# Three chained stages on one core: layer 2 of the last stage moved, tile by tile, between layer 1's products

## The chip, the cores and the metric

One core of a Trainium2 chip runs the whole program in one launch. The metric is device time in microseconds (us). TensorE (PE) multiplies, VectorE (DVE) and ScalarE (ACT) move and combine data, GpSimd (POOL) combines data and issues one of the DMA queues, SyncE (SP) issues the other. An engine works through its instructions in the order of the program.

## The reference, cut to what matters

```python
x = attention(q_l, k_l, v_l, q_g, k_g, v_g)       # 4 x 544 tokens = 2176 rows of 512
x = x + gate * (relu(x @ w1[e]) @ w2[e])           # one of 8 experts e per row, some rows skipped
out = ((x @ w_a) * (x @ w_b)) @ w_out              # 512 -> 1536 -> 512: the stage that is changed
```

Everything is float32. The last line is the last stage; a float32 product is made there of three products of a high and a low part (high by high, high by low, low by high).

## The kernel before

Attention and routing run first, then the experts, then the last stage (class `Late`), which begins at about 307 us of the span and fills the rest. It runs under a schedule written out by hand, so the order of every engine's instructions is that of the code.

The last stage holds the 1536 hidden columns in 12 slices of 128. Six groups g take two slices each (`NM` is 12). Within a group four steps go over four blocks of rows (`TILES`: three of 4 tiles of 128 rows, and block 3 with 5), in the order 0, 1, 2, 3 in even groups and 3, 2, 1, 0 in odd ones. A step (`step`) makes the layer 1 products by seven half-size products per slice in place of eight (a Strassen-like scheme): product numbers 0, 4, 5, 1, 6, 2, 3, each for the slices j = 0 and 1, and each six matmuls into one of three PSUM banks per slice. Between them ACT copies a bank (`cp`, line 562) and DVE adds and multiplies (lines 590, 603, 598), and the result goes as high and low parts into the four tiles `g` (lines 562 and 594). The first two steps of group 0 are plain products (`plain_step`).

Layer 2 (`second`, line 516) multiplies the `g` tiles of the step before by the two slices of `w_out` (tiles `wo`, high and low), six 512-column matmuls for each 128 rows of output, into one of two PSUM banks (`accs`). ACT copies the bank to an `o` buffer (line 519), and the buffer goes to `out`: in group 0 by a plain store on SP's queue, in the later groups by an adding DMA on POOL's queue (line 524). In `step` all tiles of the step before are made one behind the other, between product 4 and product 5 (hook `P5`, then `s0` to `s3`, then `s`). There are two `o` buffers until the end of step 2 of group 1, where `all_o` adds four in the tiles `raws[3]` and `raws[4]`.

`aux(g, s)` says what else is issued at each hook (`P0`, `P1`, ... name the product that comes next): `conv` unpacks a loaded slice of weights (three DVE instructions, lines 317 to 319) and issues the next load on SP; `sums` (three DVE instructions) and `hi`, `lo` make the seven weight combinations in high and low parts; `wo_hi`, `wo_lo` do that for `w_out`; `turns` transposes rows on PE through the `accs` banks and `build` (`x_parts`) makes the seven combinations of a block's rows. Blocks 0 and 3 share one slot, so they are written to memory (`spill_x`, SP's queue: all of block 3 at `P5` of step 3 of group 0, all of block 0 at the end of step 2 of group 1) and read back (`fill_x`, POOL's queue) in groups 2 to 5: three pieces in step 1, at `s`, `P2` and `end`, the fourth at `s` of step 2. The block read back is used in step 3.

Of the kernel before, what the change touches and what calls it, by code (L numbers as in the profile page):

```python
# [8 lines left out]
F32 = mybir.dt.float32  # L9
# [5 lines left out]
ALU = mybir.AluOpType  # L15
# [210 lines left out]
class Late:  # L226
# [8 lines left out]
    def __init__(self, ctx, tc, dram, ident, wa, wb, wo, x2d, out, st):  # L235
        self.ctx, self.tc, self.nc = ctx, tc, tc.nc
        self.ident, self.x2d, self.out, self.st = ident, x2d, out, st
        self.src = (wa, wb, wo)
        self.es = ExitStack()
        self.xd = {b: [dram.tile([128, 7, 2 * self.NW[b]], F32, name=f"xd{b}{z}") for z in "hl"] for b in (0, 3)}  # L240
        self.todo = [(m, k) for g in range(0, self.NM, 2) for m, k in ((g, 0), (g, 1), (g + 1, 0), (g + 1, 1), (g, 2), (g + 1, 2))]
        self.ready, self.rows = [], {}
        self.nraw = self.nout = self.npair = 0

    def pool(self, name, es=None):
        return (es or self.es).enter_context(self.tc.tile_pool(reuse_waits="tile", name=name, bufs=1))

    def open_shared(self):

        self.xr_p = self.es.enter_context(self.tc.tile_pool(reuse_waits="tile", name="xr", bufs=6))  # L250
        p = self.pool("late_g")
        self.g = [p.tile([128, 640], F32R, name=f"g{z}") for z in range(4)]
        self.tmp = [p.tile([128, 640], F32, name=f"tmp{z}") for z in range(2)]
        self.idf = p.tile([128, 1], F32, name="idf")

    def open_first(self):

# [29 lines left out]
        self.xf_es.close()  # L287
        self.slots.append(self.slot(self.pool("late_w2"), 2))

    def all_o(self):  # L290
        self.o += [self.raws[3 + z // 2][:, 512 * (z % 2):512 * (z % 2) + 512] for z in range(4)]


    def fetch(self, raw, m, k):
# [186 lines left out]
            else:  # L481
                tt(a12, a12, a11, ALU.subtract)

    def spill_x(self, b):
        for z, x in enumerate(self.xview(b)):
            for a, e in ((0, 3), (3, 7)):
                self.nc.sync.dma_start(self.xd[b][z][:, a:e], x.bitcast(F32)[:, a:e].rearrange("p a k n -> p a (k n)"))

    def fill_x(self, b, z, a, e):
        x = self.xview(b)[z]  # L490
# [7 lines left out]
    def product(self, j, m, b, wp, xp, bank, start):  # L498
# [4 lines left out]
        for z, (w, x, k) in enumerate(terms):  # L503
            self.nc.tensor.matmul(bank[:, 0:n], lhsT=w[:, k], rhs=x[:, xp, k], start=start and z == 0, stop=z == 5,  # L504
                                  skip_group_check=not start)

    def second(self, b, g):

        nc = self.nc
        for q, t in enumerate(self.TILES[b]):  # L510
            acc = self.acc()
            for j in range(2):
                gh, gl = (x[:, 128 * q:128 * q + 128] for x in self.g[2 * j:2 * j + 2])
                wh, wl = self.wo[j]
                for z, (a, w) in enumerate(((gh, wh), (gh, wl), (gl, wh))):
                    nc.tensor.matmul(acc, lhsT=a, rhs=w, start=(j == 0 and z == 0), stop=(j == 1 and z == 2))  # L516
            o = self.o[self.nout % len(self.o)]
# [35 lines left out]
    def step(self, g, b, prev, run):  # L553
# [60 lines left out]
    def aux(self, g, s):  # L614
# [21 lines left out]
        more = 2 * g + 2 < self.NM  # L636
        c0, c1 = slice(0, 128), slice(128, 256)
        if (g, s) == (0, 0):
            add("p00", conv, conv)
            add("p01", do(self.turn_plain, 1, 0), do(self.turn_plain, 1, 1))  # L640
            add("p10", wo_hi, do(self.turn_plain, 1, 2), do(self.turn_plain, 1, 3), do(self.load_x, 2), do(self.sums, 0))
            add("p11", *his[2:])
            add("end", wo_lo, *los[2:])
        elif (g, s) == (0, 1):
            add("p0", *turns(2, 0, 1))
            add("p00", *turns(2, 2, 3), do(self.load_x, 3))
            build(2, ("p00", "s0", "s1", "s2", "s3", "p01", "p10"))
            add("p01", do(self.sums, 1))
            add("p10", *his[2:])
            add("p11", *los[2:])  # L650
        elif (g, s) == (0, 2):
            add("P0", *turns(3, 0, 1))
            add("P1", *turns(3, 2, 3))
            add("P5", *turns(3, 4), do(self.load_x, 1))
            build(3, ("P5", "s0", "s1", "s2", "s3", "s", "P6"))
            add("P6", conv)
            add("P2", conv)
        elif (g, s) == (0, 3):
            add("P5", do(self.open_slot2), do(self.spill_x, 3), sums)
            add("s0", *his)  # L660
            add("s1", *los)
            add("s2", conv)
            add("s3", conv)
            add("s", sums)
            add("P6", H(0, 1), H(4, 5), H(5, 6))
            add("P2", L(0, 1), L(4, 5), L(5, 6), H(1, 2))
            add("P7", L(1, 2), H(6, 7))
            add("P3", H(2, 3))
        if g and s == 0:
            add("P1", H(3, 4))  # L670
            add("P5", L(6, 7), L(2, 3))
            add("s0", L(3, 4))
            if g < 3:
                add("s3", conv)
                add("s4" if g == 1 else "s3", conv)
            add("s", wo_hi)
            add("P6", wo_lo)
        if (g, s) == (1, 0):
            add("P0", *turns(1, 0, 2, w=128, xf=0))
            build(1, ("P1", "P5", "s0", "s1", "s2", "s3", "s4"), c0, 0)  # L680
            add("end", do(self.load_x, 0))
        elif (g, s) == (1, 1):
            add("P0", *turns(1, 1, 3, w=128, xf=0))
            build(1, ("P1", "P5", "s0", "s1", "s2", "s3", "s4"), c1, 0)
            add("s3", *turns(0, 0, w=128, xf=1))
            add("s4", *turns(0, 2, w=128, xf=1))
            build(0, ("s", "P6", "P2", ((1, 2), "P1"), ((1, 2), "P5"), ((1, 2), "s0"), ((1, 2), "s1")), c0, 1)
        elif (g, s) == (1, 2):
            add("P1", *turns(0, 1, 3, w=128, xf=0))
            build(0, ("s0", "s1", "s2", "s3", "s", "P6", "P2"), c1, 0)  # L690
            add("s", conv)
            add("P6", conv)
            add("end", do(self.spill_x, 0), do(self.all_o))
        elif (g, s) == (1, 3):
            add("P1", sums)
            add("P5", *his)
            add("s0", *los)
            add("s1", conv)
            add("s2", conv)
            add("s3", sums)  # L700
            add("s", H(0, 1), H(4, 5))
            add("P6", L(0, 1), L(4, 5), H(5, 6))
            add("P2", L(5, 6), H(1, 2))
            add("P7", L(1, 2), H(6, 7))
            add("P3", H(2, 3))
        if g > 1 and more:
            if s == 1:
                add("P5", conv)
                add("s0", conv)
                add("s1", sums)  # L710
                add("s2", *his)
                add("s3", *los)
            elif s == 2:
                add("P5", conv)
                add("s1", conv)
            elif s == 3:
                add("P0", sums)
                add("P1", H(0, 1))
                add("P5", H(4, 5))
                add("s0", L(0, 1), L(4, 5))  # L720
                add("s1", conv)
                add("s2", conv)
                add("P6", H(5, 6))
                add("P2", L(5, 6), H(1, 2))
                add("P7", L(1, 2), H(6, 7))
                add("P3", H(2, 3))
        if g > 1 and s in (1, 2):
            for k, z, a, e in (("s", 0, 0, 3), ("P2", 1, 0, 3), ("end", 0, 3, 7)) if s == 1 else (("s", 1, 3, 7),):
                add(k, do(self.fill_x, (3, 0)[g % 2], z, a, e))
        return A  # L730

    def run(self):
        nc, tc = self.nc, self.tc
        with ExitStack() as ps:
# [3 lines left out]
            self.bk = [(bank[2], bank[0], bank[3]), (bank[6], bank[1], bank[4])]  # L738
            self.accs, self.nacc = (bank[5], bank[7]), 0
            self.zeroed, self.A = False, {}  # L740
            prev = None
            for g in range(self.NM // 2):
                for s, b in enumerate(self.ORDER[g % 2]):
# [897 lines left out]
```

## Time and profile before

| | us |
|---|---|
| median of 3 runs (759.27 to 761.83) | 760.81 |
| the profiled execution, its own time | 761.96 |
| its span | 760.2 |
| PE busy in the span | 705.7 (93%) |
| DVE, ACT, POOL busy | 470.9, 401.9, 170.0 |

The span runs from the first to the last instruction, and all positions below are us from its start. PE is busy for 93% of it, but the share is a mean over stages: the stretches in which PE stood still, and what ended each of them, say where time can go. The granted clock of PE is 1.00 at its full level and 0.50 at its half.

### The profile page before, as it was taken

How to read it: one execution, taken by the hardware profiler on the slowest of the kernel's cores; microseconds unless marked ns; L12 is line 12 of the kernel's file. 1: busy time of each engine (PE TensorE's matmuls, PEld its weight loads, DVE VectorE, ACT ScalarE, POOL GpSimd, SP SyncE). 2: the span in 40 equal slices, each digit the busy share in tenths (PEclk: the TensorE clock that was granted, in tenths of full speed). 3: DMA queues.
4: the chain of work that ended last, by engine and by line, in shares of the span. 5: the costliest groups of instructions: out<-in, count | busy, mean ns of one | idle time of the engine just before them, and what ended most of it. 6: DMA issues, size and time to landing. Idle time of an engine off the chain costs nothing.

```text
span 760.2 us, 14495 instructions
## 1 busy us (share of the span) xinstructions
PE 705.7 (93%) x5362; PEld 628.1 (83%) x5364; DVE 470.9 (62%) x1288; ACT 401.9 (53%) x994; POOL 170.0 (22%) x206
## 2 busy tenths in 40 slices
PE   8999998989989999889789889998999999999993
PEld 6887886868879888678689778997999899999982
DVE  6777886756565787676767469645465657533221
ACT  6776676616555784366365445534443444444332
POOL 3002022821343452000000112231222113222311
PEclk9999999899999999999989999999999999999997
DMA  9687633869977837732834478795659649745964
GB/s 302 201 252 237 204 129 111 265 222 371 370 253 247 270 107 241 242 111 98 324 107 160 68 150 269 165 314 141 106 120 277 170 58 293 161 69 71 224 122 59
DMA packets 76754, 145.53 MB, mean 191 GB/s; under 512 B 7319, under 2 KB 36759, under 8 KB 75140
## 3 DMA queue, kind: packets, MB, share of 16 engines
q1 hardware_dynamic: 58820, 101.78, 40.3%
q0 software_dynamic: 16784, 42.71, 26.1%
q8 instruction: 44, 0.72, 0.4%
q14 instruction: 34, 0.28, 0.1%
q10 hardware_dynamic: 1072, 0.04, 0.1%
HBM read 96.78 MB, written 51.18 MB: 195 GB/s over the span
## 4 chain that ended last, share of the span: by engine, by line
PE 56%; issue 15%; DVE 10%; DMA 7%; ACT 7%; POOL 4%; SPq 0%; POOLq 0%; ACTq 0%; DVEq 0%
PE bank L504 17%; PE bank L516 11%; PE acc L1372 7%; PE ph L220 4%; POOL out L524 3%; PE ph L212 3%; ACT sm L901 3%; PE o L931 3%; DMA out<-o 3%; PE bank L538 2%; PE sps L885 2%; PE tps L914 1%; DVE sm L897 1%; PE xp L953 1%; DMA xl<-xd0l 1%
## 5 line engine op out<-in xcount | busy, mean ns | idle before, releaser
L504 PE MATMUL bank<-xh,w 128*128 128x256 f32 (+1 forms) x1232 | 244.0, 293 | 9.0 <-ACT tmp L562 5.4
L504 PEld LDWEIGHTS bank<-xh,w 128*128 128x128 f32 x1232 | 200.2, 193 | 10.8 <-ACT tmp L562 5.9
L504 PE MATMUL bank<-xl,w 128*128 128x256 f32 (+1 forms) x616 | 180.6, 293 | 6.0 <-DMA xl<-xd0l 3.3
L516 PE MATMUL bank<-woh,g 128*128 128x512 f32 x408 | 133.5, 397 | 2.4 <-ACT o L519 2.0
L504 PEld LDWEIGHTS bank<-xl,w 128*128 128x128 f32 x616 | 118.8, 193 | 7.9 <-DMA xl<-xd0l 3.7
L516 PEld LDWEIGHTS bank<-woh,g 128*128 128x128 f32 x408 | 76.8, 188 | 21.6 <-ACT o L519 3.1
L562 ACT ACTIVATE g<-tmp 128x256 fp32r<-128x256 f32 (+1 forms) x88 | 38.1, 433 | 106.0 <-DVE tmp L598 106.0
L171 DVE TENSOR_TENSOR lo<-raw,hi 128x1024 fp32r<-128x1024 f32 x47 | 64.2, 1376 | 34.0 <-ACT hi L161 33.5
L516 PE MATMUL bank<-wol,g 128*128 128x512 f32 x204 | 80.6, 395 | 0.0
L524 POOL DMA_DIRECT2D out<-raw x52 | 45.2, 880 | 151.2 <-ACT raw L519 147.2
L161 ACT ACTIVATE hi<-raw 128x1024 fp32r<-128x1024 f32 x60 | 63.4, 1058 | 28.4 <-issue 12.8
L524 POOL DMA_DIRECT2D out<-o x33 | 29.0, 887 | 206.5 <-ACT xh L472 113.1
L590 DVE TENSOR_TENSOR tmp<-bank,tmp 128x256 f32<-128x256 f32 (+1 forms) x44 | 19.3, 442 | 79.6 <-PE bank L504 79.5
L901 ACT ACTIVATE sm<-sm,nm 128x224 f32<-128x224 f32 (+1 forms) x128 | 58.3, 457 | 15.5 <-DVE nm L897 15.5
L171 POOL TENSOR_TENSOR lo<-raw,hi 128x1024 fp32r<-128x1024 f32 x17 | 41.6, 2448 | 59.6 <-ACT hi L161 59.3
L519 ACT ACTIVATE raw<-bank 128x512 f32<-128x512 f32 x52 | 31.1, 598 | 40.5 <-PE bank L516 40.4
L519 ACT ACTIVATE o<-bank 128x512 f32<-128x512 f32 x50 | 29.6, 597 | 42.2 <-PE bank L516 24.1
L562 ACT ACTIVATE tmp<-bank 128x256 f32<-128x256 f32 (+1 forms) x88 | 33.4, 398 | 22.7 <-PE bank L504 19.4
L516 PEld LDWEIGHTS bank<-wol,g 128*128 128x128 f32 x204 | 38.4, 188 | 8.1
L1137 POOL DMA_INDIRECT xs<-xt,slu x16 | 16.8, 1047 | 115.7 <-DMA vt<-v 62.0
L1372 PE MATMUL acc<-hi,hl 128*128 128x512 f32 x88 | 36.4, 414 | 6.5 <-DVE hl L1360 6.3
L594 DVE TENSOR_TENSOR g<-tmp,g 128x256 fp32r<-128x256 f32 (+1 forms) x88 | 38.4, 436 | 3.3 <-ACT g L562 1.5
(261 smaller groups left out, 1413.3 us busy)
## 6 DMA issues: line engine op xcount, KB each, us to landing
raw<-w SPq DMA_DIRECT2D x64, 512.0 KB, 6.4
out<-raw POOLq DMA_DIRECT2D x52, 256.0 KB, 6.6
out<-o POOLq DMA_DIRECT2D x33, 256.0 KB, 5.1
vt<-v SPq DMA_DIRECT2D x16, 512.0 KB, 4.7
raw<-qk SPq DMA_DIRECT2D x14, 576.0 KB, 5.5
xr<-x2d SPq DMA_DIRECT2D x25, 256.0 KB, 2.8
raw<-wa SPq DMA_DIRECT2D x12, 512.0 KB, 6.4
raw<-wb SPq DMA_DIRECT2D x12, 512.0 KB, 4.5
```

Of the source, the lines that this page charges most:

```text
L161: nc.scalar.activation(hi, rv, AF.Copy)
L171: eng.tensor_tensor(lo, rv, hi.bitcast(F32), ALU.subtract)
L212: nc.tensor.matmul(ph, lhsT=w[:, d, 128 * j:128 * j + 128], rhs=x[:, d, :], start=(z == 0), stop=(z == 11))
L220: nc.tensor.matmul(ph, lhsT=x[:, d, :], rhs=w[:, d, :], start=(z == 0), stop=(z == 11))
L504: self.nc.tensor.matmul(bank[:, 0:n], lhsT=w[:, k], rhs=x[:, xp, k], start=start and z == 0, stop=z == 5, skip_group_check=not start)
L516: nc.tensor.matmul(acc, lhsT=a, rhs=w, start=(j == 0 and z == 0), stop=(j == 1 and z == 2))
L519: nc.scalar.activation(o, acc, AF.Copy)
L524: nc.gpsimd.dma_start(dst, o, accum_op=ALU.add)
L562: cp = lambda o, i: nc.scalar.activation(o, i, AF.Copy)
L594: tt(g4[2 * j + 1][:, h], (u, p)[h][j], g4[2 * j].bitcast(F32)[:, h], ALU.subtract)
L901: st_.exp = nc.scalar.activation(sm[:, j, :cn], sm[:, j, :cn], AF.Exp, bias=nm[:, hh, j:j + 1], scale=-1.0, accum_out=dens[p][:, hh, i:i + ...
L1372: nc.tensor.matmul(acc, lhsT=a[:, j, c], rhs=w[:, j, :], start=(q == 0 and j == 0 and z == 0), stop=(q == NQ - 1 and j == 1 and z == 2))
```

## The change

- `second` is taken one tile at a time. After product 4 comes tile 0, after product 5 tile 1, after product 1 the extra tile of a block with five, after product 6 the next, after product 2 the last. The hooks of `aux` move with it: what was issued between tiles is now issued around the products, `wo_lo` moves behind the step's last product, one `conv` of group 0 moves from step 2 to step 3, and in the plain steps `wo_lo` moves ahead of the weight sums and the combinations `hi`, `lo` of the first slice move to the next step.
- Four `o` buffers from the start (`more_o(3)`), two in steps 1 and 2 of group 1 (where `raws` hold rows), then six.
- Group 0's stores go out on POOL's queue as well, plain, and the adding DMAs of later groups wait by name for the store before of the same rows.
- In the last group the sums so far are read back on SP's queue into the `o` buffer up to four tiles ahead (`fetch_sums`), DVE adds the bank to them, and SP stores the result; ACT's copy and the adding DMA fall away for these 17 tiles.
- `spill_x` goes out in four pieces, at `P5`, `P2` and `P3` of the same step (step 3, for block 0 too) and at `P1` of the next. `fill_x` goes out in step 1 alone: two pieces at `P0`, one at `P7`, one at the end.
- `idf` grows from 4 to 64 bytes per partition, and a 32 byte tile `edge` is put in front of the experts' `h` and `xt` tiles. What is opened behind them moves by 32 bytes.

```diff
-        self.idf = p.tile([128, 1], F32, name="idf")
+        self.idf = p.tile([128, 16], F32, name="idf")[:, 0:1]
...
-    def all_o(self):
-        self.o += [self.raws[3 + z // 2][:, 512 * (z % 2):512 * (z % 2) + 512] for z in range(4)]
+    def more_o(self, *r):
+        self.o[2:] = [self.raws[z][:, c:c + 512] for z in r for c in (0, 512)]
...
+    def fetch_sums(self, last):
+        while self.tile_of and self.tile_of[0][0] <= last:
+            n, t = self.tile_of.pop(0)
+            o = self.sums_in[n] = self.o[n % len(self.o)]
+            ld = self.nc.sync.dma_start(o, self.out[128 * t:128 * t + 128, :])
+            after(self.tc, ld, [self.written[t]])
...
-            nc.scalar.activation(o, acc, AF.Copy)
-            dst = self.out[128 * t:128 * t + 128, :]
-            if g == 0:
+            if g == self.NM // 2 - 1:
+                self.fetch_sums(n + 4)
+                o = self.sums_in.pop(n)
+                nc.vector.tensor_tensor(o, acc, o, ALU.add)
                 nc.sync.dma_start(dst, o)
             else:
-                nc.gpsimd.dma_start(dst, o, accum_op=ALU.add)
+                o = self.o[n % len(self.o)]
+                nc.scalar.activation(o, acc, AF.Copy)
+                i = nc.gpsimd.dma_start(dst, o, accum_op=ALU.add if g else ALU.bypass)
+                if g:
+                    after(self.tc, i, [self.written[t]])
+                self.written[t] = i.ins.name
+                if n + 1 == self.tile_of[0][0]:
+                    self.fetch_sums(n + 4)
...
         run("P5")
-        for q in self.second(*prev):
-            run(f"s{q}")
-        run("s")
+        sec = self.second(*prev)
+        next(sec)
+        run("s0")
...
         run("P6")
+        next(sec)
+        run("s1")
...
         run("P2")
+        if len(self.TILES[prev[0]]) > 4:
+            next(sec)
...
         run("P7")
+        next(sec)
+        run("s2")
...
         run("P3")
+        next(sec)
+        run("s3")
...
...
         elif (g, s) == (0, 3):
-            add("P5", do(self.open_slot2), do(self.spill_x, 3), sums)
-            add("s0", *his)
+            add("P1", conv)
+            add("P5", do(self.open_slot2), sums)
+            add("P6", *his)
             add("s1", *los)
-            add("s2", conv)
-            add("s3", conv)
-            add("s", sums)
+            add("s1", conv)
+            add("P2", conv)
+            add("P2", sums)
...
-            add("s", wo_hi)
-            add("P6", wo_lo)
+            add("s3", wo_hi)
+            add("end", wo_lo)
...
-        if g > 1 and s in (1, 2):
-            for k, z, a, e in (("s", 0, 0, 3), ("P2", 1, 0, 3), ("end", 0, 3, 7)) if s == 1 else (("s", 1, 3, 7),):
+        if g > 1 and s == 1:
+            for k, z, a, e in (("P0", 0, 0, 3), ("P0", 1, 0, 3), ("P7", 0, 3, 7), ("end", 1, 3, 7)):
                 add(k, do(self.fill_x, (3, 0)[g % 2], z, a, e))
...
+        rows_es.enter_context(tc.tile_pool(name="edge", bufs=1, side="right")).tile([128, 8], F32, name="edge")
```

## Rows read from the trace of the kernel before

**Rows 1.** Stretches: us; busy us (instructions) per engine; PE clock; DMA share, GB/s.

```profile
344.40:460.00 115.60, 103.00 (x647) 93.65 (x646) 78.53 (x171) 61.09 (x144) 9.08 (x11) 0.97 0.56 163
460.00:748.30 288.30, 282.21 (x1843) 260.81 (x1842) 149.60 (x337) 125.84 (x287) 72.74 (x90) 0.99 0.70 164
```

**Rows 2.** Who PE waited for, 307 to 748: us, times, longest.

```profile
PE bank L504 <- ACT tmp L562: 5.4, 2, 3.6
PE bank L504 <- DVE tmp L590: 3.6, 2, 2.0
PE bank L504 <- DMA xl<-xd0l: 3.3, 2, 1.7
PE bank L504 <- DMA xl<-xd3l: 2.8, 2, 2.6
PE bank L516 <- ACT o L519: 2.0, 3, 1.4
PE bank L438 <- ACT xf L451: 1.8, 1, 1.8
PE bank L438 <- ACT o L519: 1.6, 1, 1.6
```

**Rows 3.** Stretches of 5 us with their granted clock, columns as in rows 1.

```profile
360.00:365.00 5.00, 3.05 (x26) 2.84 (x25) 4.83 (x10) 0.33 (x1) 0.00 (x0) 1.00 0.54 123
380.00:385.00 5.00, 2.98 (x11) 2.98 (x12) 1.59 (x4) 3.48 (x9) 0.00 (x0) 0.55 0.53 176
520.00:525.00 5.00, 4.71 (x18) 4.39 (x19) 0.68 (x2) 1.18 (x3) 0.00 (x0) 0.66 0.00 0
```

**Rows 4.** The chain that ended last: start us, us, what, instructions.

```profile
335.93 8.19 PE bank L538 x36
382.02 7.90 PE bank L504 x36
...
471.68 5.60 PE bank L516 x24
477.28 10.07 PE bank L504 x84
...
664.24 12.31 PE bank L504 x84
```

**Rows 5.** Who ACT waited for, 307 to 748: us, times, longest.

```profile
ACT o L519 <- DMA out<-o: 18.1, 8, 7.3
```

**Rows 6.** DVE's instructions in order of time, at 363 and 478.

```profile
363.10 0.75 DVE L590 TENSOR_TENSOR tmp<-bank,tmp 128x256 f32<-128x256 f32 x2
...
478.46 1.29 DVE L397 TENSOR_TENSOR wol<-pair,woh 128x512 fp32r<-128x512 f32 x2 [3.28 <-ACT woh L392]
```

**Rows 7.** ACT at 382 (group 0), DVE and ACT in a step of group 2.

```profile
382.48 0.73 ACT L367 ACTIVATE w<-t 128x256 fp32r<-128x256 f32 x2
...
483.22 0.41 DVE L603 TENSOR_TENSOR tmp<-bank,tmp 128x256 f32<-128x256 f32 x1
...
484.12 0.42 ACT L562 ACTIVATE g<-tmp 128x256 fp32r<-128x256 f32 x1 [0.37 <-DVE tmp L598]
```

**Rows 8.** DMA issues, 307 to 748: KB each, median us to landing.

```profile
out<-raw POOLq DMA_DIRECT2D x51, 256.0 KB, 6.6
out<-o POOLq DMA_DIRECT2D x33, 256.0 KB, 5.1
...
out<-o SPq DMA_DIRECT2D x17, 256.0 KB, 4.1
```

**Rows 9.** The end: PE's last product, POOL's last issue, two stretches as in rows 1.

```profile
747.85 0.40 PE L516 MATMUL bank<-woh,g 128*128 128x512 f32 x1
749.23 0.86 POOL L524 DMA_DIRECT2D out<-raw  x1 [0.53 <-ACT raw L519]
...
750.00:755.00 5.00, 0.00 (x0) 0.00 (x0) 0.00 (x0) 0.00 (x0) 0.09 (x1) 0.75 0.80 125
755.00:760.00 5.00, 0.00 (x0) 0.00 (x0) 0.00 (x0) 0.00 (x0) 0.00 (x0) 0.50 0.00 0
```

More of the change, by code (lines that the diff above doesn't have):

```diff
@@ L482, in x_parts, with spill_x @@
                 tt(a12, a12, a11, ALU.subtract)
[L484 to L487, printed above, removed]
+    def spill_x(self, b, z, a, e):
+        x = self.xview(b)[z]
+        self.nc.sync.dma_start(self.xd[b][z][:, a:e], x.bitcast(F32)[:, a:e].rearrange("p a k n -> p a (k n)"))
     def fill_x(self, b, z, a, e):
@@ L638, in aux @@
         if (g, s) == (0, 0):
+            self.more_o(3)
             add("p00", conv, conv)
             add("p01", do(self.turn_plain, 1, 0), do(self.turn_plain, 1, 1))
-            add("p10", wo_hi, do(self.turn_plain, 1, 2), do(self.turn_plain, 1, 3), do(self.load_x, 2), do(self.sums, 0))
-            add("p11", *his[2:])
-            add("end", wo_lo, *los[2:])
+            add("p10", wo_hi, do(self.turn_plain, 1, 2), do(self.turn_plain, 1, 3), do(self.load_x, 2), wo_lo)
+            add("p11", do(self.sums, 0))
         elif (g, s) == (0, 1):
             add("p0", *turns(2, 0, 1))
-            add("p00", *turns(2, 2, 3), do(self.load_x, 3))
+            add("p00", *turns(2, 2, 3), do(self.load_x, 3), *his[2:])
+            add("s0", *los[2:])
             build(2, ("p00", "s0", "s1", "s2", "s3", "p01", "p10"))
@@ L673, in aux @@
             if g < 3:
[L674 to L677 removed]
+                add("P2", conv)
+                add("P2" if g == 1 else "P2", conv)
+            add("s3", wo_hi)
+            add("end", wo_lo)
         if (g, s) == (1, 0):
[L679 to L680 removed]
+            add("P1", *turns(1, 0, 2, w=128, xf=0))
+            build(1, ("P5", "s0", "P6", "s1", "P2", "P7", "s2"), c0, 0)
             add("end", do(self.load_x, 0))
         elif (g, s) == (1, 1):
[L683 to L687, printed above, removed]
+            self.more_o()
+            add("P1", *turns(1, 1, 3, w=128, xf=0))
+            build(1, ("P5", "s0", "P6", "s1", "P2", "P2", "P7"), c1, 0)
+            add("P2", *turns(0, 0, w=128, xf=1))
+            add("P2", *turns(0, 2, w=128, xf=1))
+            build(0, ("P2", "P7", "s2", ((1, 2), "P1"), ((1, 2), "P5"), ((1, 2), "s0"), ((1, 2), "P6")), c0, 1)
         elif (g, s) == (1, 2):
             add("P1", *turns(0, 1, 3, w=128, xf=0))
[L690 to L693, printed above, removed]
+            build(0, ("s0", "P6", "s1", "P2", "P2", "P7", "s2"), c1, 0)
+            add("P2", conv)
+            add("P7", conv)
+            add("end", do(self.more_o, 3, 4))
         elif (g, s) == (1, 3):
@@ L697, in aux @@
             add("s0", *los)
+            add("P6", conv)
             add("s1", conv)
[L699 to L705, printed above, removed]
+            add("P2", sums)
+            add("P2", H(0, 1), H(4, 5))
+            add("P7", L(0, 1), L(4, 5), H(5, 6))
+            add("s2", L(5, 6), H(1, 2))
+            add("P3", L(1, 2), H(6, 7))
+            add("s3", H(2, 3))
         if g > 1 and more:
@@ L709, in aux @@
                 add("s0", conv)
-                add("s1", sums)
-                add("s2", *his)
-                add("s3", *los)
+                add("P6", sums)
+                add("s1", *his)
+                add("P2", *los)
             elif s == 2:
                 add("P5", conv)
-                add("s1", conv)
+                add("P6", conv)
             elif s == 3:
@@ L720, in aux @@
                 add("s0", L(0, 1), L(4, 5))
+                add("P6", conv)
                 add("s1", conv)
[L722 to L726, printed above, removed]
-        if g > 1 and s in (1, 2):
-            for k, z, a, e in (("s", 0, 0, 3), ("P2", 1, 0, 3), ("end", 0, 3, 7)) if s == 1 else (("s", 1, 3, 7),):
+                add("P7", H(5, 6))
+                add("s2", L(5, 6), H(1, 2))
+                add("P3", L(1, 2), H(6, 7))
+                add("s3", H(2, 3))
+        if (g, s) in ((0, 3), (1, 3)):
+            for k, z, a, e in (("P5", 0, 0, 3), ("P2", 1, 0, 3), ("P3", 0, 3, 7), ((g + 1, 0), 1, 3, 7)):
+                add(k if type(k) is str else "P1", do(self.spill_x, (3, 0)[g], z, a, e), at=None if type(k) is str else k)
+        if g > 1 and s == 1:
+            for k, z, a, e in (("P0", 0, 0, 3), ("P0", 1, 0, 3), ("P7", 0, 3, 7), ("end", 1, 3, 7)):
                 add(k, do(self.fill_x, (3, 0)[g % 2], z, a, e))
@@ L740, in run @@
             self.zeroed, self.A = False, {}
+            order = [t for b in self.ORDER[(self.NM // 2 - 1) % 2] for t in self.TILES[b]]
+            self.tile_of = [(NT * (self.NM // 2 - 1) + z, t) for z, t in enumerate(order)]
             prev = None
```

19 lines of the change are left out of this document (10 added, 9 removed).

## The prediction

> **What bounds the kernel now.** I read the table of stretches first [rows 1]: from 460 us on PE is busy for 282.21 of 288.3 us, between 344 and 460 for 103.00 of 115.6. So the last stage is set by PE, and a change in order can only win what PE stood still, what it lost by a lower clock, and what lies behind its last product. The list of PE's waits says what the standing still was [rows 2]. In groups 0 and 1: 5.4 us for ACT's copies of a bank that the next product adds to, 3.6 for DVE's addition at line 590, 2.0 and 1.6 for ACT's copy to an `o` buffer, 1.8 for ACT's copies of transposed rows; together 14.4. In groups 2 to 5, four waits for a refill of the shared block: 3.3 and 2.8, together 6.1. There is nothing else worth naming.
>
> Two of these waits cost twice. After the wait of 3.6 us the granted clock is at 0.55 in 380 to 385, after the one of 2.6 it is at 0.66 in 520 to 525, between the full level and the half one (2.4 and 1.2 GHz); after the wait of 2.0 at 363 it stays at 1.00 [rows 3]. The chain prices the first: 36 products of 320 columns took 7.90 us, where 84 take 12.31, so 36 are worth 5.28, a loss of 2.6 [rows 4]. The second: the clock's shortfall is 0.34 of 5 us, 1.7.
>
> **What ACT and DVE were late with.** ACT stood 18.1 us waiting for an `o` buffer whose store had not landed, 7.3 in one piece [rows 5]. That piece is in step 3 of group 0, where the stores stand in SP's queue behind the whole spill of block 3. ACT works in order, so the bank copies that PE needs stand behind the blocked copy. DVE's addition at line 590 came at 363.10 [rows 6], behind two `conv`, while product 3, which needs the bank, followed product 6 by only one product pair.
>
> **The change, part by part.**
>
> *Tiles between products.* The number of products stays, and so does their time: a pair takes 12 of 84 parts of 10.07 us, 1.44, a tile a quarter of 5.60, 1.40 [rows 4]. In that row of the chain tile and product follow each other without a gap (471.68 + 5.60 = 477.28), so I take nothing for three more changes between the two per step. What moves is slack. From product 6 to product 3 it was 1.44 us and becomes 1.44 + 2 x 1.40 = 4.2; from product 5 to 6, 1.44 becomes 2.8, and 4.2 with a block of five. From product 4 to 5, 5.6 becomes 1.4: ACT must copy four banks there at some 0.4 each, which begin when the step before has given its last `g` (about 1.7 us into the step), so they end at about 3.3, and product 5 begins at 4.3. It holds with 1 us to spare; were it not so, each step would lose what is missing.
>
> *Stores.* With four `o` buffers from the start, and stores off the queue that carries the spills, ACT isn't blocked in group 0. In steps 1 and 2 of group 1 there are still two. A buffer is then busy for 0.6 (copy) + 0.9 (issue) + 5.1 (landing) = 6.6 us [rows 8, 9], and the same buffer comes up again after two tiles, that is 2 x 1.40 + 3 x 1.44 = 7.1 us. It just fits; before, it came up after 2.8. So the waits for `o` go, with the 3.6 and 1.8 us behind them.
>
> *What stays.* DVE is busy for 78.53 of 115.6 us there [rows 1], and its work isn't less; one `conv` even moves into step 3 of group 0, which now has three, two `sums` and four `lo`. I laid DVE's queue by hand beside PE's new order, from the rows' durations: addition 590 is late by 0.4 us in that step, product 0 of the next step by 1.3 (its bank is still being read), again by 1.1 where group 2 begins, the second half of `wo_lo`, which now ends only as the next step's tile 0 begins, by 0.8 in group 1 (1.29 us behind the last `lo` [rows 6]), and tile 2 of the second plain step by 0.8 behind ACT's weight combinations. Sum 4.4; I take 5. From below 0; from above 12, if DVE comes out as far behind as in the rows before. Each is under 2 us, so I count no loss of clock with them (the wait of 2.0 had none). That makes 14.4 + 2.6 - 5.0 = 12.0 us won.
>
> *Refills.* The last piece moves from the middle of step 2 to the end of step 1, ahead by some 8 us, and the first by as much; they move past the adding stores of that step on POOL's queue. All four waits were under 3 us, so I take all: 6.1 + 1.7 = 7.8. What is late next are the step's stores behind two refills in the same queue; with six buffers a buffer comes up again after one and a half steps, over 20 us. Without that cover ACT would block as in group 0.
>
> *Last group.* 17 reads of 256 KB and 17 plain stores come to SP's queue, 17 adding DMAs leave POOL's. A DVE addition of 512 columns (0.69) takes the place of a copy on ACT, four per step of 15.7 us: hidden. The added wait is SP's for the group's earlier sums to land; behind it in that queue are only other such reads and the stores, since all weights have been loaded, and a read is issued four tiles before DVE wants it, some 15 us.
>
> *The end.* PE ends at 748.25, the last adding DMA was issued at 749.23, moved data until about 754 (0.80 of the stretch from 750) and the span ended at 760.2 [rows 9]. Now: last product, addition 0.7, then a plain store, 4.1 us to landing under load [rows 8]: 753.1 against about 754, so at least 1 won. The 5 us from 755 on show no work [rows 9]; if winding up POOL's own DMAs is in them, up to 5 more can go, since POOL's last one now is a refill 40 us earlier. Between 1 and 6 I take 4.5, nearer to 6, as POOL has nothing under way then.
>
> *32 bytes.* By the order in which tiles are opened, each rounded up to 32 bytes, the weight slots, the rows and `wo` begin on a multiple of 64 bytes and the `g` tiles halfway between two; afterwards all lie halfway. Of 512-column products, those that take both operands from the first kind ran at 8.19 / 36 = 0.2275 us, those of `second`, which mix the kinds, at 5.60 / 24 = 0.2333 [rows 4]. If that is the mixing, 612 of them gain 612 x 0.0058 = 3.5 us; if it isn't, nothing. Products of 256 columns keep like beside like. I take 3. In the experts' stage both kinds change sides; I take nothing.
>
> **Sum.** 12.0 + 7.8 + 4.5 + 3.0 = 27.3. The profiled execution took 761.96, so 734.7; the median of the runs shown is 1.15 below it, so 733.5.
>
> **Rivals.**
>
> *DVE is the bound in groups 0 and 1.* For it: its share there, and the three `conv` in one step. Against: 37 us of 115 idle. Then 10 more come back: 743.5. Chance 0.12.
>
> *Refills are late by their rate, not by their issue.* The DMA share from 460 on is 0.70, and near full for pieces of it; against it, 8 us of lead against waits of at most 2.6. Then 7.8 stay: 741.3. Chance 0.07.
>
> *POOL's stores land too late for two buffers.* In groups 2 to 5 an adding DMA of the same size took 6.6 us, not 5.1 [rows 8]; then a buffer is busy for 8.1 us against 7.1, 1 us late at some eight tiles, half of it on PE's path: 737.5 to 741.5. Group 0's own stores took 4.1 on SP. Chance 0.06. The Trainium skill, on its page "DMA: Bandwidth & Descriptors", section "Issuing engine by pattern", gives simple loads and stores to SyncE and holds its queue to be the faster in general, which speaks against moving group 0's stores; the rows agree on the order (4.1 against 5.1), and by that rule alone four buffers still hide the difference.
>
> *Slower: the last tiles wait for the new `g`.* The tile behind product 2 reads the second half of the `g` tiles just after ACT has been told to write the first half. If the waits are set for whole tiles, it waits for the addition, product and copy behind product 2: from 483.22 to 484.54 they took 1.3 us [rows 7], with the signals on both sides some 1.4 (an estimate), in 22 steps 31 us: 733.5 + 31 = 764.5. It decides from 1.25 us per step on. Against it: ACT wrote parts of a weight slot at 382.48 [rows 7] while products of the same step still had to read other parts of it, so waits go by parts. Chance 0.04.
>
> *The waits only move.* If the new order gives every wait back elsewhere, only the end and the alignment could show, and a delay of the reads could eat these: 760. Chance 0.03.
>
> **How the numbers follow.** The forecast has 0.68, with a range of its own of 726 to 740: no residual wait gives 728.5, an end of 6 another 1.5 less; no gain from the padding gives 736.5, an end of only 1 gives 737, both 740. With the first three rivals (0.25), which reach up to 743.5, and 3 us on either side for what rows of another order can't price, the range is 723 to 746. Differences under 0.3% (2.3 us) can't be told from no change with this kernel. Faster by more: 0.68 + 0.12 + 0.07 + 0.06 = 0.93; within 0.3%: 0.03; slower: 0.04.
>
> **What would show it.** In the changed profile ACT should have hardly a wait for the landing of `out`; PE's waits for ACT's bank copies and for addition 590 should be under 2 us each, and mostly at the seam of groups 0 and 1; none for a refill; the clock at 1.00 from 315 to 748; 24 products of `second` in 5.46 us rather than 5.60; less than 8 us behind the last product. A wait of 1.4 us before the last tile of every step would make the prediction wrong, and so would DVE's queue running a whole product pair behind in groups 0 and 1, or DVE in the last group waiting for the sums read back.

## The result and the profile after

The changed kernel took 722.57 us (median of 4 runs, 719.78 to 724.96), the kernel before beside it 760.04; the ratio is 0.9488, 95% interval 0.9439 to 0.9536. The forecast was 733.5, with a range of 723.0 to 746.0: the sign holds, the gain is 10.9 us larger than said, and the time lies 0.4 us under the range. The profiled execution took 724.27 us, its span is 722.2.

The spans differ by 38.0 us. I cut both, in order of time, at the first product of the plain steps, at that of step 2 of group 0, at that of step 0 of group 2, and at the end of the last product of layer 2:

| us | before | after | won | forecast |
|---|---|---|---|---|
| ahead of the last stage | 307.6 | 304.4 | 3.2 | 0 |
| two plain steps | 37.6 | 34.7 | 2.9 | 13.0 with the next row |
| rest of groups 0 and 1 | 123.4 | 107.1 | 16.3 | |
| groups 2 to 5 | 279.6 | 269.7 | 9.9 | 9.8 |
| behind the last product | 11.9 | 6.4 | 5.5 | 4.5 |

The forecast column is the prediction's sum, with a third of the padding's 3.0 us put to the first two groups of six: 12.0 + 1.0, then 7.8 + 2.0.

Stretches of after, columns as in rows 1: the rest of groups 0 and 1, then groups 2 to 5.

```profile
339.06:446.16 107.10, 106.70 (x708) 99.11 (x706) 85.21 (x189) 65.02 (x154) 17.45 (x25) 1.00 0.64 178
446.16:715.82 269.66, 269.66 (x1778) 250.74 (x1776) 154.08 (x336) 113.33 (x262) 57.92 (x72) 1.00 0.77 192
```

PE is busy for 106.70 of 107.10 us and then without any gap; in the two stretches of [rows 1] it idled 12.6 and 6.1. The granted clock is 1.00 in both. The list of PE's waits from 304 to 722 us answers to [rows 2] (us, times, longest) and is complete:

```profile
PE bank L554 <- DVE xl L424: 0.8, 1, 0.8
PE bank L524 <- ACT o L534: 0.5, 1, 0.5
PE bank L524 <- ACT xf L452: 0.3, 1, 0.3
PE bank L524 <- ACT raw L452: 0.2, 1, 0.2
```

1.8 us in all; no refill is in it, no bank copy (now L578), no addition (now L610). The chain that ended last shows the new order (columns as in [rows 4]):

```profile
550.02 1.39 PE bank L524 x6
551.41 1.42 PE bank L504 x12
...
710.31 5.52 PE bank L524 x24
```

A tile is worth 1.39 us, a product pair 1.42, as cut from [rows 4]; one follows the other without a gap (550.02 + 1.39 = 551.41). The last 24 products took 5.52 us, not the 5.46 forecast, against 5.60.

The adding and plain stores of POOL, which answer to [rows 8] (count, KB each, median us to landing), land sooner than the 6.6 and 5.1 us of before:

```profile
out<-raw POOLq DMA_DIRECT2D x48, 256.0 KB, 4.3
out<-o POOLq DMA_DIRECT2D x37, 256.0 KB, 4.2
```

The end, in order of time: the last product, then the addition that took the place of ACT's copy; below, two stretches.

```profile
715.42 0.40 PE L524 MATMUL bank<-woh,g 128*128 128x512 f32 x1
715.86 0.69 DVE L530 TENSOR_TENSOR raw<-bank,raw 128x512 f32<-128x512 f32 x1 [0.68 <-PE bank L524]
```

```profile
716.00:720.00 4.00, 0.00 (x0) 0.00 (x0) 0.55 (x1) 0.00 (x0) 0.00 (x0) 0.95 0.39 139
720.00:722.20 2.20, 0.00 (x0) 0.00 (x0) 0.00 (x0) 0.00 (x0) 0.00 (x0) 0.50 0.02 7
```

Cut by single us, the DMA share is 0.23 in 718 to 719, 0.00 in 719 to 720 and at most 0.04 after it: some 3 us remain almost without a transfer, where the kernel before had 5 to 6 (0.04 in 754 to 755, then 0.00 [rows 9]).

### The profile page after: what moved, and what is told of

Same layout as the page of the kernel before. It is cut to its first block, busy times and chain, and to the rows that moved or that the text cites. A ratio compares the mean times of both kernels' runs of the same rounds, so it can differ in the third digit from the quotient of the medians.

```text
span 722.2 us, 14521 instructions
## 1 busy us (share of the span) xinstructions
PE 693.2 (96%) x5362; PEld 623.1 (86%) x5364; DVE 485.3 (67%) x1305; ACT 392.7 (54%) x977; POOL 164.4 (23%) x206
## 4 chain that ended last, share of the span: by engine, by line
PE 77%; DVE 10%; ACT 7%; DMA 3%; issue 1%; SPq 0%; DVEq 0%; ACTq 0%
PE bank L504 31%; PE bank L524 19%; PE acc L1404 7%; PE ph L220 4%; ACT sm L932 4%; PE ph L212 3%; PE bank L554 3%; PE o L962 3%; PE sps L916 1%; DVE lo L171 1%; DMA raw<-w 1%; DVE sm L928 1%; PE bank L439 1%; PE xp L984 1%; ACT gsm L1025 1%
## 5 line engine op out<-in xcount | busy, mean ns | idle before, releaser
L504 PE MATMUL bank<-xh,w 128*128 128x256 f32 (+1 forms) x1232 | 251.5, 290 | 0.1
L504 PE MATMUL bank<-xl,w 128*128 128x256 f32 (+1 forms) x616 | 178.4, 290 | 0.0
L524 PE MATMUL bank<-woh,g 128*128 128x512 f32 x408 | 143.6, 395 | 1.1 <-ACT o L534 0.5
L504 PEld LDWEIGHTS bank<-xl,w 128*128 128x128 f32 x616 | 116.1, 188 | 4.2
L171 DVE TENSOR_TENSOR lo<-raw,hi 128x1024 fp32r<-128x1024 f32 x47 | 66.4, 1423 | 35.4 <-ACT hi L161 33.6
L578 ACT ACTIVATE g<-tmp 128x256 fp32r<-128x256 f32 (+1 forms) x88 | 37.8, 432 | 69.7 <-DVE tmp L620 68.9
L535 POOL DMA_DIRECT2D out<-raw x48 | 39.1, 814 | 139.8 <-ACT raw L534 121.6
L610 DVE TENSOR_TENSOR tmp<-bank,tmp 128x256 f32<-128x256 f32 (+1 forms) x44 | 18.8, 441 | 58.3 <-PE bank L504 58.2
L534 ACT ACTIVATE raw<-bank 128x512 f32<-128x512 f32 x48 | 28.6, 595 | 51.6 <-PE bank L524 50.6
L578 ACT ACTIVATE tmp<-bank 128x256 f32<-128x256 f32 (+1 forms) x88 | 34.6, 399 | 25.7 <-PE bank L504 22.2
L620 DVE TENSOR_TENSOR tmp<-bank,tmp 128x256 f32<-128x256 f32 (+1 forms) x88 | 38.9, 442 | 11.7 <-PE bank L504 10.2
L1404 PE MATMUL acc<-hi,hl 128*128 128x512 f32 x88 | 36.3, 413 | 6.7 <-DVE hl L1392 6.3
```

The source lines that it names most:

```text
L171: eng.tensor_tensor(lo, rv, hi.bitcast(F32), ALU.subtract)
L535: i = nc.gpsimd.dma_start(dst, o, accum_op=ALU.add if g else ALU.bypass)
L578: cp = lambda o, i: nc.scalar.activation(o, i, AF.Copy)
L620: tt(v, (b1, b2)[h][j][:, 0:n], v, ALU.mult)
L1404: nc.tensor.matmul(acc, lhsT=a[:, j, c], rhs=w[:, j, :], start=(q == 0 and j == 0 and z == 0), stop=(q == NQ - 1 and j == 1 and z == 2))
```

## The experiments

Twelve kernels, in three groups of four, each group beside runs of the kernel before on its own chip. The table cuts their traces as above; "second" and "experts" are the mean ns from start to start of two neighbouring 512-column products of layer 2 and of the experts' L1404, pairs with a wait between them left out. The ratio is to the kernel before on the same chip, which took 760.0 beside after, then 763.2, 759.7 and 760.9 beside the three groups (each group's kernels stand together); so times of different groups compare by their ratios.

| kernel | ahead | plain | 0, 1 | 2 to 5 | end | second | experts | median us | ratio, 95% |
|---|---|---|---|---|---|---|---|---|---|
| before | 307.6 | 37.6 | 123.4 | 279.6 | 11.9 | 233.2 | 232.5 | 760.0 | 1 |
| after | 304.4 | 34.7 | 107.1 | 269.7 | 6.4 | 230.3 | 230.1 | 722.6 | 0.949 (0.944 to 0.954) |
| after_again | 306.4 | 36.3 | 107.1 | 269.7 | 6.8 | 230.4 | 230.0 | 726.1 | 0.952 (0.948 to 0.956) |
| no_padding | 307.7 | 36.3 | 107.2 | 270.1 | 6.7 | 232.8 | 232.4 | 729.3 | 0.956 (0.952 to 0.960) |
| padding_alone | 310.9 | 36.0 | 124.9 | 277.3 | 12.6 | 229.2 | 229.7 | 760.2 | 0.995 (0.992 to 0.998) |
| late_refills | 306.6 | 34.7 | 107.1 | 274.4 | 6.4 | 230.4 | 229.9 | 731.1 | 0.958 (0.953 to 0.963) |
| adding_dma | 301.8 | 34.8 | 107.1 | 269.7 | 10.6 | 230.4 | 230.0 | 726.7 | 0.959 (0.954 to 0.964) |
| last_store_pool | 302.4 | 34.7 | 107.1 | 269.7 | 10.8 | 230.3 | 229.8 | 727.6 | 0.960 (0.955 to 0.965) |
| tiles_in_a_run | 303.8 | 37.5 | 129.3 | 269.7 | 6.4 | 229.7 | 229.9 | 744.9 | 0.982 (0.976 to 0.987) |
| two_buffers_sp | 304.3 | 36.1 | 107.1 | 269.7 | 5.6 | 230.3 | 229.7 | 722.6 | 0.952 (0.947 to 0.957) |
| order_only | 306.9 | 34.7 | 113.5 | 274.7 | 12.8 | 232.7 | 232.3 | 741.7 | 0.975 (0.972 to 0.979) |
| two_bufs_spill_at_once | 305.8 | 35.5 | 113.5 | 269.7 | 5.9 | 230.4 | 229.8 | 729.7 | 0.960 (0.956 to 0.963) |
| all_but_order | 303.1 | 37.5 | 120.0 | 269.5 | 6.5 | 229.2 | 229.8 | 736.0 | 0.967 (0.964 to 0.971) |
| like_at_64 | 305.8 | 34.7 | 107.1 | 269.7 | 6.7 | 230.4 | 232.4 | 725.6 | 0.953 (0.950 to 0.957) |

Read down a column: groups 0 and 1, and 2 to 5, repeat to 0.2 us where an edit doesn't touch them, while the time ahead of the stage runs from 301.8 to 310.9 in code that hardly differs, and the end from 5.6 to 6.8 where SP stores last. The traces tell where; the medians carry that chance.

### Which part freed groups 0 and 1

**all_but_order**: the old order, with everything else of the change.

```diff
         run("P5")
-        sec = self.second(*prev)
-        next(sec)
-        run("s0")
+        for q in self.second(*prev):
+            run(f"s{q}")
+        run("s")
...
-            build(3, ("P5", "s0", "P6", "s1", "P2", "P2", "P7"))
-            add("end", conv)
+            build(3, ("P5", "s0", "s1", "s2", "s3", "s", "P6"))
+            add("P6", conv)
+            add("P2", conv)
```

> The changed kernel with the order of the kernel before, tiles in one run and side work at its old places; padding, early refills, four o buffers, POOL's stores in group 0, spread spills and sums read back stay. Theory one, the order is what removed the waits in groups 0 and 1: 3 us for the padding, 5.3 for the end and 5 to 8 for the refills are all that is won, 743 to 747. Rival, ACT no longer blocked is most of it: the waits in groups 0 and 1 shrink from 20 us with the clock to under 10, 732 to 738.

PE's waits in the last stage (us, times, longest; addition 590 is L606 here):

```profile
PE bank L504 <- DVE tmp L606: 3.6, 2, 1.9
PE bank L524 <- ACT o L534: 2.2, 3, 1.5
PE bank L504 <- ACT tmp L578: 1.8, 1, 1.8
PE bank L439 <- ACT xf L452: 1.8, 1, 1.8
PE bank L439 <- ACT o L534: 1.6, 1, 1.6
```

These are the rows of [rows 2] again, but for the bank copy of 3.6 us: 11.0 us of waits, and the stretch of groups 0 and 1 is 12.9 us longer than after's, 3.4 shorter than before's. So theory one is right about most of what these groups won. ACT still waits 8.0 us for the landing of out, with four buffers, but in four pieces of at most 2.7. The total came out where the rival had it for other reasons: groups 2 to 5 won 10.1 us, more than theory one had put down, and the part ahead of the stage, which neither had in its sum, is 4.5 us shorter in this trace.

**order_only** is the opposite, the old kernel in the new order; **two_bufs_spill_at_once** and **two_buffers_sp** are the changed kernel with group 0's stores as before, with and without both spills issued whole ahead of them:

```diff
-            self.more_o(3)
...
-                i = nc.gpsimd.dma_start(dst, o, accum_op=ALU.add if g else ALU.bypass)
+                i = nc.gpsimd.dma_start(dst, o, accum_op=ALU.add) if g else nc.sync.dma_start(dst, o)
...
-            for k, z, a, e in (("P5", 0, 0, 3), ("P2", 1, 0, 3), ("P3", 0, 3, 7), ((g + 1, 0), 1, 3, 7)):
+            for k, z, a, e in (("P5", 0, 0, 3), ("P5", 0, 3, 7), ("P5", 1, 0, 3), ("P5", 1, 3, 7)):
```

> The kernel before with the new order alone: tiles between the products, and the side work at its new places; two o buffers, group 0's stores on SP's queue behind the whole spill, late refills, adding DMAs to the end, no padding. Theory one, the order removes the waits in groups 0 and 1 by itself (20 us with the clock behind them, less some 2): 760 - 18 = about 742, from the first product of the plain step to the end of the last 420 to 423 us rather than 440.7, with 3 to 8 us of refill waits left in it. Rival, the order and the free o buffers are needed together: ACT stands 7 us for a buffer in step 3 of group 0 and PE behind it, 748 to 752.

> The changed kernel with two o buffers and SP's queue for group 0's stores, and with both spills issued whole behind product 4, ahead of those stores. Theory one, with a tile every 2 to 4 us nobody needs the buffer at once, and what ACT is late is covered: 723 to 725 beside 722.6 for the same with the spill spread. Rival, the spill in front of the stores is what blocked ACT: 5 us or more of its waiting for the landing of out in step 3 of group 0, PE waits of 3 to 6 us with the clock behind them, 727 to 731.

> The changed kernel with two o buffers in group 0 and its stores on SP's queue, as before, the spill spread over the step as now. Theory one, interleaving: a buffer comes up again only after 7 us, so the stores land in time except behind a piece of the spill; under 3 us, 723 to 726. Rival, the buffers did it: ACT waits 7 us or more for an o buffer in step 3 of group 0 and PE behind it 4 to 8 us, 727 to 731.

The table gives 113.5, 113.5 and 107.1 us for groups 0 and 1, where the kernel before took 123.4: of the 16.3 us won there the new order alone brings 9.9, the spill in pieces the other 6.4. order_only took what theory one said, 741.7, with the rival's block inside it: ACT waited 7.7 us in one piece, PE 4.1 behind it. What ACT and PE waited for in two_bufs_spill_at_once, and its stretches around it (columns as in rows 1):

```profile
ACT o L534 <- DMA out<-o: 8.6, 3, 7.2
```

```profile
PE bank L439 <- ACT o L534: 3.6, 2, 2.9
```

```profile
375.00:380.00 5.00, 3.39 (x21) 2.76 (x19) 2.15 (x6) 0.00 (x0) 0.00 (x0) 1.00 1.00 412
380.00:385.00 5.00, 2.89 (x12) 2.50 (x13) 3.19 (x8) 4.24 (x12) 0.00 (x0) 0.63 0.81 299
385.00:390.00 5.00, 5.00 (x23) 4.64 (x22) 2.36 (x8) 3.48 (x9) 0.00 (x0) 0.69 0.00 1
```

ACT's block of 7.3 us [rows 5] is back at 7.2. PE then waits 3.6 us for ACT, and the clock is at 0.63 and 0.69 in the two stretches from 380 on, between its levels of 2.4 and 1.2 GHz. The wait and this shortfall (at most 3.4 us) account for the 6.4 us. In two_buffers_sp ACT waits 1.3 us in all for the landing of stores from its o buffers, and PE not behind it. So the rival for two_bufs_spill_at_once is right and the one for two_buffers_sp wrong: given the new order, the spill in pieces is enough to free ACT, and the two more buffers and POOL's queue add nothing to it. Whether these two would have been enough beside a spill issued whole, no run shows.

**tiles_in_a_run** takes the tiles out from between the products and leaves all side work at its new places:

```diff
         sec = self.second(*prev)
-        next(sec)
+        for q in sec:
+            pass
         run("s0")
```

> The changed kernel with all tiles of layer 2 in one run behind product 4, as before; every other piece of work keeps its place among the products of layer 1. Theory one, the interleaving gives ACT and DVE the slack that removed the waits in groups 0 and 1: the waits for ACT's bank copies and for DVE's addition in front of product 3 come back, 6 to 12 us in groups 0 and 1 with the clock behind them, little in groups 2 to 5; 729 to 735. Rival, the o buffers and the spread of the spill did it (ACT was blocked, nothing else): under 3 us, 723 to 726.

```profile
PE bank L504 <- DVE tmp L607: 8.0, 4, 3.7
PE bank L524 <- ACT o L534: 2.5, 3, 1.6
PE bank L504 <- ACT tmp L578: 2.3, 1, 2.3
PE bank L504 <- DVE tmp L616: 2.2, 3, 1.8
```

PE waits most for the addition in front of product 3 (8.0 us), and groups 0 and 1 take 129.3 us, 5.9 more than in the kernel before. It came out 10 us above the upper end of what theory one said: in groups 0 and 1, new places for the side work without the tiles between them are worse than the old kernel, not as good. Groups 2 to 5 took the same 269.7 us.

### Refills

**late_refills**:

```diff
-        if g > 1 and s == 1:
-            for k, z, a, e in (("P0", 0, 0, 3), ("P0", 1, 0, 3), ("P7", 0, 3, 7), ("end", 1, 3, 7)):
+        if g > 1 and s in (1, 2):
+            for k, z, a, e in (("P2", 0, 0, 3), ("s2", 1, 0, 3), ("end", 0, 3, 7)) if s == 1 else (("P2", 1, 3, 7),):
```

> The changed kernel with the refills issued where they were in time: the first when half the step's products are done, the last in the middle of the step before the reads. Theory one, the lead of their issue is what counts: PE waits again some 5 to 6 us in all for the refilled block in groups 2 to 5, and loses clock behind the longest, so 722.6 + 7 = about 729.5. Rival, the waits came from the stores that stood ahead of them in POOL's queue, of which two per step are now issued later and those of the last group are gone: under 2 us of waits, 723 to 724.5.

PE's waits for refills, and the stretches around the longer one:

```profile
PE bank L504 <- DMA xl<-xd3l: 2.7, 2, 1.9
```

```profile
495.00:500.00 5.00, 3.13 (x22) 2.87 (x21) 3.25 (x8) 2.00 (x5) 0.59 (x1) 0.97 0.93 249
500.00:505.00 5.00, 5.00 (x23) 4.58 (x23) 2.33 (x5) 2.04 (x5) 0.24 (x1) 0.69 0.04 7
```

Groups 2 to 5 take 4.7 us more: 2.7 of waits and the rest in the clock, at 0.69 behind the longer. Both theories get half. The waits for block 3 come back with the late issue, those for block 0 (3.3 us in [rows 2]) don't. In order_only, where group 5 still has its adding DMAs, they are gone as well, so the new order alone removes them; what in it does so, I haven't separated.

### The end

**adding_dma** copies and adds the last group's tiles as before; **last_store_pool** keeps the read-back and DVE's addition, and changes one queue:

```diff
                 nc.vector.tensor_tensor(o, acc, o, ALU.add)
-                nc.sync.dma_start(dst, o)
+                nc.gpsimd.dma_start(dst, o)
```

> The changed kernel with the last group's tiles copied by ACT and added by POOL's DMAs, as in the groups before it: nothing is read back. Theory one, the 5.5 us won behind the last product are the end of POOL's own queue: from the end of the last product to the end of the span 11 to 12 us rather than 6.4, the rest unchanged, so 722.6 + 5.3 = about 728. Rival, the end is the landing of the last transfer whatever it is: 1 us more, about 723.6.

> The changed kernel with the last group's sums read back and added by DVE as now, but the plain stores issued by POOL. It parts the adding DMA from POOL's queue. Theory one, having a DMA of POOL's own under way at the end is what costs: 10.5 to 12 us behind the last product, about 727.5. Rival, the adding (its read and write in the DMA) costs: 7 us behind the last product, about 723.

Stretches behind the last product, which ended at 713.86 in last_store_pool; columns as in rows 1.

```profile
716.00:720.00 4.00, 0.00 (x0) 0.00 (x0) 0.00 (x0) 0.00 (x0) 0.00 (x0) 0.78 0.21 75
720.00:724.70 4.70, 0.00 (x0) 0.00 (x0) 0.00 (x0) 0.00 (x0) 0.00 (x0) 0.50 0.00 0
```

A plain store from POOL leaves 10.8 us behind the last product, an adding DMA 10.6, a store from SP 5.6 to 6.8. Cut by single us, last_store_pool's DMA share is 0.11 in 717 to 718 and 0.00 from 718 on: its data had landed, and 6.7 us without work follow. In adding_dma the share is still 0.72 in 718 to 719, that is 4.7 to 5.7 us behind the last product at 713.32, and 0.01 in the next us. So the plain store's data lands sooner and the span ends no sooner: it isn't the adding that costs at the end but that POOL's own DMA is the last, some 4 to 5 us. What POOL's queue does in that time the profile doesn't show. The Trainium skill, page "DMA: Bandwidth & Descriptors", section "Issuing engine by pattern", gives simple stores to SyncE; the runs agree here by these 4 to 5 us. In group 0, where the same rule spoke against the change, they show no cost (two_buffers_sp, 107.1 us either way).

### The padding

```diff
-        self.idf = p.tile([128, 16], F32, name="idf")[:, 0:1]
+        self.idf = p.tile([128, 1], F32, name="idf")
...
-        rows_es.enter_context(tc.tile_pool(name="edge", bufs=1, side="right")).tile([128, 8], F32, name="edge")
```

is **no_padding**; **padding_alone** is the kernel before with these two lines of the change; **like_at_64** is the changed kernel without "edge" and with 32 bytes ahead of the g tiles:

```diff
+        p.tile([128, 8], F32, name="ahead")
         self.g = [p.tile([128, 640], F32R, name=f"g{z}") for z in range(4)]
...
-        rows_es.enter_context(tc.tile_pool(name="edge", bufs=1, side="right")).tile([128, 8], F32, name="edge")
```

> The changed kernel without the two pieces of padding, so that the weight slots, the shared rows and wo begin again on a multiple of 64 bytes and the g tiles halfway between. Theory one, the placing sets the pace of a product: a 512-column product of layer 2 goes back from 230.3 to 233.2 ns, one of the experts from 230.1 to 232.5, the time rises by 3.1 us (1.6 in the last stage, 1.5 in the experts), to about 725.7. Rival, the pace came from elsewhere (the new order, the clock): products stay at 230.3, time as for the changed kernel, 722.6.

> The kernel before with the two pieces of padding and nothing else. Theory one, the placing sets the pace: products of layer 2 at 230.3 rather than 233.2 ns, of the experts at 230.1 rather than 232.5; 760.0 - 3.1 = 757. Rival, it does nothing by itself: 760.

> The changed kernel with 32 bytes put in front of the g tiles rather than behind them, and none in front of the rows of the experts: then the g tiles and wo, slots and rows all begin on a multiple of 64 bytes, and the experts' two operands lie unlike again. Theory one, a product is slower when its operands lie unlike, wherever they lie: products of layer 2 at 230.3 ns, of the experts at 232.4. Rival, it is the multiple of 64 that is slow (or the place of the weights alone): layer 2 at 233, experts at 232.4.

One group of layer 2's products (mean ns of one behind the bar) in no_padding, then in like_at_64:

```profile
L524 PE MATMUL bank<-wol,g 128*128 128x512 f32 x204 | 80.6, 395 | 0.0
```

```profile
L525 PE MATMUL bank<-wol,g 128*128 128x512 f32 x204 | 80.1, 392 | 0.0
```

395 ns where, by the order in which tiles are opened, the operands lie unlike, as before; 392 where they lie alike, here both on a multiple of 64. From start to start it is 232.8 against 230.4, and the experts' products, alike in after and unlike in like_at_64, go from 230 to 232.4. So it is the mixing that is slow, not the place, as the prediction had guessed. What it is worth is less sure. The medians are 3.0 us apart with the old order (padding_alone against before, interval 0.2 to 0.8%) and 3.2 with the new (no_padding against after_again, whose intervals overlap). In the traces the stage of no_padding is only 0.5 us longer than after_again's, and about 1 more lies in the experts (below); the rest I can't place.

The traces show why the stage gains so little. In groups 2 to 5 the 68 tiles, each from its first product to whatever follows its last, take 95.4 us in before and 93.5 in padding_alone, but 94.6 in no_padding and 94.2 in after_again: the padding wins 1.9 us there with the old order and 0.4 with the new. In the new order every tile is followed by a product of layer 1, and that one starts 227.7 ns behind the tile's last product where the operands of layer 2 lie unlike, 233.0 where they lie alike, which gives back part of what is won inside a tile. So the gains of the padding and of the new order don't add up.

### after_again

> The changed kernel as it is, once more: a yardstick for the runs beside it. 720 to 725 us, 0.945 to 0.953 of the kernel before. Question: the first product of the plain step came at 304.4 us in the first trace of it, at 307.6 in that of the kernel before. Theory one, the padding makes the products of the experts faster (1.5 us) and the rest is chance: 304 to 307 here. Rival, all of it is chance: as likely 306 to 309.

It reached the last stage at 306.4, which settles nothing by itself; the 301.8 to 310.9 of all traces do: most of the 3.2 us won ahead of the stage in the first trace is chance. What the padding gives there is about 1 us: 264 products by 2.4 ns are 0.6, and 310 of L220, whose mean went from 117.5 ns in before to 116.2 in after, give 0.4. The first stretch of the stage, in after, after_again and before:

```profile
304.40:309.40 5.00, 4.22 (x17) 3.27 (x18) 4.93 (x9) 1.98 (x4) 0.86 (x1) 1.00 0.38 112
```

```profile
306.40:311.40 5.00, 4.21 (x10) 3.09 (x11) 4.93 (x10) 1.42 (x3) 0.89 (x1) 0.67 0.38 109
```

```profile
307.60:312.60 5.00, 4.22 (x11) 3.17 (x12) 4.93 (x10) 1.40 (x3) 0.88 (x1) 0.66 0.37 113
```

The same code finds the clock at 1.00, its full level of 2.4 GHz, or at 0.67, between the levels of 2.4 and 1.2 GHz; hence 34.7 or 36.3 us for the plain steps. In the 5 us ahead of it PE was busy for 3.69 and 3.35 us, at 1.00 in both. The trace of the kernel before had the low one, so another 1.6 us of the first comparison are chance, and the other 1.3 of the 2.9 won there are the order's. The ratios, 0.952 for after_again against 0.949, fit this, though their intervals overlap.

No run points to a version faster than the changed kernel: PE has no gap left from 446 us on. two_buffers_sp, with two `o` buffers and SP's stores in group 0, is as fast.

## Why the prediction was right in kind and too small in size

**Tiles between products: right.** No pair of tile and product costs anything, and all waits of [rows 2] in groups 0 and 1 are gone. PE waited in front of product 5 in no step.

**What stays: the step that failed.** "Sum 4.4; I take 5." The plain steps and groups 0 and 1 won 19.2 us against 13.0. Take off the 1.6 of chance at the start and some 0.5 of padding, and 17.1 remain, as much as the whole 14.4 + 2.6 that I had counted before the subtraction. The first of my five places shows why. DVE around addition 590 (L610) in step 3 of group 0, in order of time:

```profile
370.90 0.42 DVE L360 TENSOR_TENSOR t<-pair,t 128x256 f32<-128x256 f32 x1
371.24 0.88 DVE L610 TENSOR_TENSOR tmp<-bank,tmp 128x320 f32<-128x320 f32 x2
372.04 0.42 DVE L371 TENSOR_TENSOR w<-pair,w 128x256 fp32r<-128x256 f32 x1
```

Product 3, which wants the bank, starts at 372.11, and the first of the two additions is done 0.4 us sooner (371.72); I had it 0.4 late. So the layout was wrong by 0.8 us here. Of the other four places, the wait in the second plain step came, 0.5 for 0.8; product 0 of group 1 began some 0.3 us behind its pace, for 1.3, too little to stand in the list of waits; for the 1.1 and the 0.8 there is nothing. All five came out sooner than laid out, by 0.3 to 1.1 us: the layout ran late throughout, and I counted its lateness as loss, some 0.8 us measured for the 5.0 taken. Which piece of it was too long the prediction doesn't show, so that stays open. One thing that misleads can be seen: DVE's instructions overlap by some 0.08 us where one doesn't need the result of the other, so that in groups 0 and 1 of after their durations add up to 94.3 us where DVE was busy for 85.2.

**Stores: right in result, cause only in part.** ACT no longer blocks, as said; I gave that to four buffers and POOL's queue, and neither is needed: with the spill in pieces two buffers and SP's queue do as well, and with the spill whole they lose 6.4 us. The order brings 9.9 of the 16.3 by itself, and all but the order only 3.4: without the order the rest removes fewer of the waits.

**Refills: right**, 7.8 forecast. Groups 2 to 5 won 9.9, of which 1.2 are the faster tiles (95.4 against 94.2) and the other 8.7 the refills and the clock behind them. That the row met the 9.8 forecast is in part luck, since 2.0 of these were padding. Without the early issue 4.7 come back; the waits for block 0 are gone with the order alone.

**The end: 4.5 forecast, 5.5 measured**; that POOL's DMA was the last is the cause of 4.2 of it by experiment (adding_dma 10.6 against 6.4). The other 1.3, between adding_dma and before's 11.9, no run explains.

**32 bytes: right by luck.** 3.0 forecast, 3.0 and 3.2 by the medians. I had it all in layer 2 and nothing in the experts, where both operands were to change sides; their products went from 232.5 to 230.1 ns, so there too unlike became like. The traces show about 0.5 in the last stage and 1 in the experts.

The rivals fell: DVE is busy for 85.21 of 107.10 us and PE waits for it nowhere there; no refill is late; POOL's stores land in 4.2 to 4.3 us, and ACT's list has no wait for the landing of out (two of its copies to `o` buffers waited 1.0 us each for a DMA that the profile names as a refill; PE didn't wait behind them); in PE's list no tile waits for the new g; the waits didn't move elsewhere. The sum is short by 10.7 us in the traces (38.0 - 27.3): 6.2 up to the end of group 1, 3.2 ahead of the stage, 1.0 at the end, 0.1 in groups 2 to 5, and rounding. Of these some 4 are chance (1.6 by the clock at the start, about 2 ahead of the stage) and some 4 to 5 the residual that I took off.

## What to carry to other kernels

A queue laid out by hand was off by 0.3 to 1.1 us at a place here, and always in the same direction; places that come out late by no more than that are no loss to be summed, and here that sum was the largest miss. To find which part of a change pays, undo each and add each alone: the two more buffers looked like the cure for ACT's block and were worth nothing once the spill no longer stood ahead of the stores. And let the last transfer of a kernel leave by a queue other than POOL's, which was worth 4 to 5 us here.

## What the runs showed of the hardware that was not expected

- With POOL's plain store as the last DMA the span goes on for 6.7 us without a transfer (DMA share 0.00 from 718 to 724.7), with its adding DMA for some 4 to 6 (adding_dma, before), with SP's store for some 3 almost without one (0.00 to 0.04); 10.8, 10.6 and 5.6 to 6.8 us in all behind the last product.
- A 512-column product whose two operands begin on unlike halves of 64 bytes starts its successor 2 to 4 ns later (means of 232.3 to 233.2 against 229.2 to 230.4), alike at either half. Where a product of layer 1 follows it is the other way round, 227.7 against 233.0, and 68 tiles of six came out only 0.4 us apart.
- The granted clock of the stage's first 5 us was 1.00 in one execution of the changed kernel and 0.67 in another, and the plain steps took 34.7 and 36.3 us.
